# A cached-attention kernel on one core: the PE loop begins with the scores, half of K's transposes move, and ScalarE issues the first loads of x and wq

## The chip, the cores and the metric

The kernel runs on one core of a Trainium2 chip. The metric is the device time of one execution in microseconds (us). A core has five instruction queues: TensorE (PE: matmuls, and PEld, its weight loads), ScalarE (ACT), VectorE (DVE), GpSimd (POOL) and SyncE (SP). DMA transfers are started by SP and ACT here, each in a queue of its own (q1 for SP, q10 for ACT), and carried out by 16 DMA engines that both share.

## The reference

There are two independent blocks, A and B, with the same shapes: B = 16 batches, Sq = 64, D = 640, H = 32 heads, Sk = 512 cached keys, Dh = 128, all bf16.

```python
q = (x @ wq).reshape(B, Sq, H, Dh).transpose(0, 2, 1, 3)
scores = einsum("bhqd,bhkd->bhqk", q, k_cache) * Dh ** -0.5
p = softmax(scores, axis=-1)
o = einsum("bhqk,bhkd->bhqd", p, v_cache)
out = o.transpose(0, 2, 1, 3).reshape(B, Sq, H * Dh) @ wo      # A and B side by side
```

K and V are 268 MB of the 292 MB that are read.

## The kernel before

**Packs.** The work is cut into 128 packs, n = 0 to 127: four heads of two batches each, so 1 MB of K and 1 MB of V. Four packs (j = 0 to 3) make a group g for one pair of batches; eight groups make a phase of 32 packs; two phases do one block. For each pack the engines do, by the names in the code:

- PE: QP projects q (20 matmuls), S makes the scores (32), TR transposes the normalised probabilities (32), PV multiplies with V (128, or 64 where j = 3), OP multiplies with wo (8). XT transposes x once in a group (5).
- ACT: QE copies q out of PSUM, EX takes the exponentials of the four heads with their row sums, OE copies PV's result, ZO clears the sums; XE copies x out of PSUM.
- DVE: KT transposes K, two instructions for a pack (KT0 and KT1 below, line 617), RC takes the reciprocals of the row sums (RC0 for three heads, RC1 for the fourth, line 659), TE copies the transposed probabilities out of PSUM (two, line 696), OS adds the output up.
- POOL: NM normalises the probabilities with the reciprocals, one instruction for a head (line 675), WP rearranges wq for one pack position j (line 575), XC copies x.T (line 592). In the last pack NM runs on DVE.
- SP: LDK (four DMAs of 256 KB, line 552), LDV (two of 512 KB, lines 563 and 565), LDX, LDWQ, and LDWO in the first phase. ACT issues the later LDWO and the stores.

**Order.** Nothing is reordered at run time. `build_plan` gives each operation a due time, the pack number plus an offset from the table `AT` in units of a pack (lines 34 to 36). Each engine's program is its operations sorted by due time (line 169), and the dependences follow the same order (lines 172 to 189): an operation waits for the latest earlier writer of what it reads, and for the earlier readers of what it writes. So an offset that moves past another changes an engine's order; one that does not, changes nothing. SP's own order comes from a separate key (the `loads` list).

In a steady pack PE does S(n), TR(n-1), OP(n-2), QP(n+1), PV(n-1). DVE does TE(n-1), RC0(n), RC1(n), then KT0(n+2) and KT1(n+2), then TE(n).

**The loop.** PE's program is a prologue, a loop of 32 turns of four packs each, and an epilogue (`run_program`, lines 796 to 819); the other engines are unrolled. A turn begins with QP(4k) and ends with OP. A turn holds 821 matmuls, with a weight load each. At the loop's start a part of the steady order has no data yet: packs -2 and -1 are dummies over zeroed buffers (VZ, BZ and WZ on DVE, lines 134 to 136, and the memsets that stand for TE(-2), line 694, and NM(-1), line 666).

**Buffers.** K has a ring of six packs, V a ring of four, the transposed K one of two. So the load of V(n) waits for PV(n-4), and the load of K(n) for S(n-6). x has a single buffer.

**The start.** SP issues x of group 0, wq for j = 0 (640 KB in rows of 1 KB), K(0), wq for j = 1, K(1), and so on. wq is needed by WP(j) on POOL, whose order is WP(0), XC(0), WP(1), NM(-1), WP(2), NM(0), WP(3), NM(1).

**The end.** A flag shows whether a softmax without maxima was safe; `If_ne` then runs a second, general program, which these inputs do not need.

Of the kernel before, what the change touches and what calls it, by code (L numbers as in the profile page):

```python
# [6 lines left out]
F32 = mybir.dt.float32  # L7
# [13 lines left out]
class Cfg:  # L21
# [9 lines left out]
    BASE = 32  # L31
    KLEAD = 2.5
    WIDE = (0, 1, 2)
    AT = dict(XT=-2.485, XE=-2.28, XC=-0.9, QP=-0.45, QE=-0.24, KT=(-1.24, -1.0), S=0,
              EX=(0.21, 0.32, 0.43, 0.54), RC=(0.53, 0.75), NM=(0.56, 0.69, 0.82, 0.95), NMZ=(0.54, 0.55, 0.56, 0.76), TR=1.2,
              TE=(1.26, 1.39), PV=1.75, OE=(2.0, 2.06), ZO=2.11, OP=2.31, OS=2.545, LDWO=2.6, ST=3.374, WP0=-1.75, WP1=-1.6)


class Op:
# [19 lines left out]
def build_plan(dims, cfg, general):  # L59
# [6 lines left out]
    N = NPH * PH  # L66
    AT = cfg.AT
    ops = []
    loads = []
# [8 lines left out]
    def add_output(n):  # L78
        g, j = n // NJ, n % NJ
        final = n >= 0 and dims["FINAL"](g // NBP)  # L80
        for b in range(2):
            tv = n + AT["PV"]
            op = add("sp", "LDV", (n, b), tv - 0.3, [], [("v" if n >= 0 else "absent", n % cfg.NV, b)])
            loads.append((n - cfg.NV + AT["PV"] + 0.2 if n >= 0 else -99.0, 3, op))
        if n > -2:
            add("pe", "TR", n, n + AT["TR"], [("pn", i) for i in range(4)] + [("ident",)], [("B", 4), ("B", 5)])
        for b in range(2):
            add("dve", "TE", (n, b), n + AT["TE"][b], [], [("B", 4 + b), ("pT", b)])
        add("pe", "PV", n, n + AT["PV"], [("pT", 0), ("pT", 1), ("v", n % cfg.NV, 0), ("v", n % cfg.NV, 1)],
            [("B", 4), ("B", 5), ("B67",)])  # L90
        add("act", "OE", (n, 1), n + AT["OE"][0], [], [("B67",), ("oT", 1)])
        add("act", "OE", (n, 0), n + AT["OE"][1], [], [("B", 4), ("B", 5), ("oT", 0)])
        add("act", "ZO", n, n + AT["ZO"], [("zeros",)], [("B67",)])
        add("pe", "OP", n, n + AT["OP"], [("oT", 0), ("oT", 1), ("wo", j)], [("B67",)])
        if j == NJ - 1:
            bp = g % NBP
            add("dve", "OS", g, n + AT["OS"], [("acc", bp)], [("B67",), ("out_sb",) if final else ("acc", bp)])
            if final:
                add("act", "ST", g, n + AT["ST"], [("out_sb",)], [("out_dram", g)])
# [4 lines left out]
    for g in range(N // NJ + 1):  # L104
        n0 = g * NJ
        txt = n0 + AT["XT"]
        add("pe", "XT", g, txt, [("xn", g % cfg.NXN), ("ident",)], [("SB", 0)])
        if g == N // NJ:
            break
        if dims["FIRST"](g // NBP):  # L110
            add("act", "XE", g, n0 + AT["XE"], [], [("SB", 0), ("xs", g % NBP)])
            op = add("sp", "LDX", g, txt - 0.5, [], [("xn", g % cfg.NXN)])
            loads.append((txt - 3.7 if g else -7.0, 0, op))
        add("pool", "XC", g, n0 + AT["XC"], [("xs", g % NBP)], [("xT", g % cfg.NX)])
    for ph in range(NPH):
        twp = [ph * PH + j + (AT["WP1"] if ph else AT["WP0"]) for j in range(NJ)]
        for kt in range(dims["KT"] if ph else 0):
            ready = twp[-1] - PH + 0.5 if ph > 1 else NJ - 1 + AT["WP0"] + 0.5
            op = add("sp", "LDWQ", (ph, kt), twp[0] - 0.5, [], [("ws", kt, j) for j in range(NJ)])
            loads.append((ready + 0.5 + 0.5 * kt if ph == 1 else ready + 2.0 + 0.14 * PH * kt, 1, op))  # L120
        for j in range(NJ):
            w = ph * NJ + j
            n0 = ph * PH + j
            add("pool", "WP", w, twp[j], [("ws", kt, j) for kt in range(dims["KT"])], [("wqp", j)])
            if not ph:
                op = add("sp", "LDWQ", (0, j), twp[j] - 0.5, [], [("ws", kt, j) for kt in range(dims["KT"])])
                loads.append((0.9 * j - 5.2, 1, op))
            if ph:
                add("act", "LDWO", w, n0 - NJ + AT["LDWO"], [], [("wo", j)])
            else:  # L130
                loads.append((n0 - 1.9, 4, add("sp", "LDWO", w, n0 + AT["OP"] - 0.8 * NJ, [], [("wo", j)])))
# [3 lines left out]
    add("dve", "BZ", 0, -9.8, [], [("B", 4), ("B", 5), ("B67",)])  # L135
    add("dve", "WZ", 0, -9.7, [], [("wo", NJ - 2), ("wo", NJ - 1)])
    add("pool", "NM", -1, -1 + AT["NM"][3], [], [("pn", i) for i in range(4)])
    for n in range(-2, N):
        add_output(n)
        if n < 0:  # L140
            continue
        g, j = n // NJ, n % NJ
        add("pe", "QP", n, n + AT["QP"], [("xT", g % cfg.NX), ("wqp", j)], [("SB", 1)])
        add("act", "QE", n, n + AT["QE"], [], [("SB", 1), ("qs", n % cfg.NQ)])
        for i in range(4):
            op = add("sp", "LDK", (n, i), n + AT["KT"][0] - 0.9, [], [("kn", n % cfg.NK)])
            loads.append((n - cfg.NV + AT["PV"] + 0.2 - cfg.KLEAD, 2, op))
        for b in range(2):
            tk = n + AT["KT"][b]
            add("dve", "KT", (n, b), tk, [("kn", n % cfg.NK)], [("kt", n % cfg.NKT, b)])  # L150
        add("pe", "S", n, n + AT["S"], [("qs", n % cfg.NQ), ("kt", n % cfg.NKT, 0), ("kt", n % cfg.NKT, 1)],
            [("SB", i) for i in range(4)])
        for i in range(4):
            h = 4 * n + i
            te = n + AT["EX"][i]
            if general:
                add("dve", "MX", h, te - 0.002, [], [("SB", i), ("negmax", h % 4)])
            add("act", "EX", h, te, [("negmax", h % 4)] if general else [],
                [("SB", i), ("p", h % cfg.NP), ("rs", h)])
            add("pool" if n < N - 1 else "dve", "NM", h, n + (AT["NM"] if n < N - 1 else AT["NMZ"])[i], [("p", h % cfg.NP), ("recip", n % cfg.NR, i // 3)], [("pn", i)])  # L160
        for a in range(2):
            add("dve", "RC", (n, a), n + AT["RC"][a], [("rs", 4 * n + i) for i in ((0, 1, 2), (3,))[a]],
                [("recip", n % cfg.NR, a)])
# [25 lines left out]
                   and not (d.dma and op.dma and d.eng == op.eng)]  # L189

    pe = progs["pe"]
    lo = next(i for i, o in enumerate(pe) if o.kind == "QP" and o.idx == 0)
    hi = next(i for i, o in enumerate(pe) if o.kind == "QP" and o.idx == cfg.PERIOD)
    size = hi - lo
    last_qp = max(o.idx for o in pe[lo:hi] if o.kind == "QP")
    reps = 1 + (N - 1 - last_qp) // cfg.PERIOD
    step = dict(XT=cfg.PERIOD // NJ, QP=cfg.PERIOD, S=cfg.PERIOD, TR=cfg.PERIOD, PV=cfg.PERIOD, OP=cfg.PERIOD)
    for k in range(reps):
        for i in range(size):
# [5 lines left out]
    for op in ops:  # L205
        if op.kind == "OP":
            at[("OE", (op.idx, 1))].deps += [d for d in op.deps if d.kind in ("LDWO", "WZ")]
            op.deps = [d for d in op.deps if d.kind not in ("LDWO", "WZ")]
        if op.kind == "XT" and op.idx > 0:
            at[("EX", 4 * (NJ * op.idx - NJ + 1))].deps += [d for d in op.deps if d.kind == "LDX"]  # L210
            op.deps = [d for d in op.deps if d.kind != "LDX"]
        if op.kind == "QP" and op.idx > 0:
            at[("EX", 4 * op.idx - 4)].deps += [d for d in op.deps if d.kind == "WP"]
            op.deps = [d for d in op.deps if d.kind != "WP"]

    own = {"XC", "QE", "KT", "NM", "TE", "OE", "ZO", "OS", "LDV"}

# [45 lines left out]
    counts = dict(base)  # L263

    def sem_key(op):
        if op.kind == "LDV":
            return ("d_v", op.writes[0][1])
        if op.kind in LOADS:
# [160 lines left out]
def mha_kernel(nc, blocks, out, cfg=None):  # L429
# [23 lines left out]
    with contextlib.ExitStack() as es:  # L453
# [24 lines left out]
        recip = sb("recip", [128, NR, 4], F32)  # L478
        ident = sb("ident", [128, 128], BF16)
        extreme = sb("extreme", [128, 4], F32)  # L480
        good = sb("good", [128, 1], BF16)
        flag = sb("flag", [1, 1], I32)
        ps = es.enter_context(nc.psum_tensor("ps", [128, 8, 512], F32))

        sems = []
        for p, (_progs, counts, _loop) in enumerate(plans):
            sems.append({key: es.enter_context(nc.semaphore("_".join([f"p{p}"] + [str(k) for k in key])))
# [124 lines left out]

        def em_KT(e, op):
            n, a = op.idx
            dst = kt_ring[:, n % NKT, 16 * a:16 * a + 16].rearrange("p t j b k two -> p (t j) b (k two)").bitcast(F32)
            src = kn_ring[:, n % NK, a, :].bitcast(F32).rearrange("p (c h b l) -> p c h b l", h=8, b=2, l=2)
            ins = e.transpose(dst.rearrange("p c b (h l) -> p c h b l", h=8, l=2), src)  # L617
# [73 lines left out]
        def em_TE(e, op):  # L691
            n, b = op.idx
            if n == -2:
                ins = e.memset(pT_sb[:, b].rearrange("p t q -> p (t q)"), 0.0)
                return ins, ins
            ins = e.tensor_copy(pT_sb[:, b].rearrange("p t q -> p (t q)"), pt_bank(b))  # L696
            return ins, ins
# [80 lines left out]
        def emit(e, op, p, taken):  # L778
# [4 lines left out]
                attach = waits.pop()  # L783
            for s, v in waits:
                e.wait_ge(sem[s], v * units(s))
            kind = "EXG" if p and op.kind == "EX" else op.kind
            first, last = emitters[kind](e, op)
            if last is None:
# [119 lines left out]
```

## Time and profile before

| | |
|---|---|
| median of 8 runs | 749.31 us (748.43 to 751.14) |
| the profiled execution | 750.81 us, span 749.1 us |
| PE busy | 684.5 us (91%) |
| DVE, ACT, POOL busy | 527.6, 519.3, 405.3 us |
| HBM read | 292.03 MB, 393 GB/s over the span |
| idle of POOL before NM | 316.2 us, waiting for RC |
| idle of DVE before KT | 99.3 us, waiting for K's DMA |

The span is cut into 40 slices of 18.7 us. A line of digits gives an engine's busy share of each slice in tenths. The chain of waits is read from the end backwards: what released each step. Its pieces stand here in the order of time as "start, length, engine, tile, line, count"; "issue" is time in which nothing that the profile shows was waited for. SPq is SP's issuing.

### The profile page before, as it was taken

Reading aid. Unit: us, or ns where it says so; the run is one execution under the profiler, and the core shown is the slowest. Engines: PE = TensorE matmul, PEld = TensorE weight load, DVE = VectorE, ACT = ScalarE, POOL = GpSimd, SP = SyncE. Lnnn points to the kernel's source line nnn. Section 1 sums busy time; section 2 is a strip of 40 time slices with the busy share of each in tenths; the row PEclk is TensorE's granted clock in tenths of the full one; section 3 lists DMA queues with packets and bytes.
Section 4 is the critical chain, followed back from the end, with each engine's and each line's share of the span. In section 5 each row is a group of like instructions: output and inputs, shape, how many; then the busy total and the mean of one; then the engine's idle time right before and its main releaser. Section 6 shows DMA issues by size and latency. Waiting matters only on the chain.

```text
span 749.1 us, 57618 instructions
## 1 busy us (share of the span) xinstructions
PE 684.5 (91%) x26518; PEld 532.8 (71%) x26518; DVE 527.6 (70%) x818; ACT 519.3 (69%) x1559; POOL 405.3 (54%) x580
## 2 busy tenths in 40 slices
PE   4679999999999999999988999999998899999995
PEld 2447777777777767767766777777776677877773
DVE  7337777777777777677756777777675787787863
ACT  2337787877767677767766777777776677777772
POOL 5425556555874554545774455455486455555550
PEclk9869999999999999999999999999999999999996
DMA  8999999999999999999999999999999999999960
GB/s 317 399 402 410 411 411 413 411 411 412 407 399 414 412 414 411 413 412 413 413 398 407 411 412 413 412 410 410 413 408 401 411 413 412 412 413 411 409 267 14
DMA packets 87518, 295.15 MB, mean 394 GB/s; under 512 B 13360, under 2 KB 28208, under 8 KB 71088
## 3 DMA queue, kind: packets, MB, share of 16 engines
q1 hardware_dynamic: 78832, 284.22, 94.9%
q10 hardware_dynamic: 8640, 10.49, 3.9%
q14 instruction: 37, 0.30, 0.1%
q8 instruction: 9, 0.15, 0.1%
HBM read 292.03 MB, written 2.62 MB: 393 GB/s over the span
## 4 chain that ended last, share of the span: by engine, by line
PE 39%; SPq 27%; DMA 12%; POOL 7%; ACT 6%; DVE 5%; issue 5%; ACTq 0%; DVEq 0%
SPq L552 18%; PE ps L710 10%; PE ps L730 10%; PE ps L603 8%; DMA kn_ring<-in_B_k_cache_dram 8%; POOL pn_sb L675 7%; PE ps L627 5%; SPq L563 5%; PE ps L686 5%; ACT p_ring L646 3%; SPq L565 3%; DMA v_ring<-in_B_v_cache_dram 2%; DMA kn_ring<-in_A_k_cache_dram 2%; DVE kt_ring L617 2%; ACT oT_sb L718 2%
## 5 line engine op out<-in xcount | busy, mean ns | idle before, releaser
L675 POOL TENSOR_SCALAR pn_sb<-p_ring,recip 128x512 bf16<-128x512 bf16 x508 | 343.1, 697 | 316.2 <-DVE recip L659 316.2
L617 DVE STREAM_TRANSPOSE kt_ring<-kn_ring 128x1024 f32<-128x1024 f32 x256 | 302.8, 1222 | 99.8 <-DMA kn_ring<-in_B_k_cache_dram 76.2
L646 ACT ACTIVATE p_ring<-ps 128x512 bf16<-128x512 f32 x512 | 298.7, 598 | 20.6 <-PE ps L627 6.1
L696 DVE COPY pT_sb<-ps 128x1024 bf16<-128x1024 bf16 x258 | 164.7, 679 | 74.8 <-PE ps L686 74.2
L710 PE MATMUL ps<-pT_sb,v_ring 32*128 32x64 bf16 (+1 forms) x14528 | 162.8, 192 | 25.5 <-DVE pT_sb L696 7.1
L710 PEld LDWEIGHTS ps<-pT_sb,v_ring 32*128 32x128 bf16 (+1 forms) x14528 | 146.4, 92 | 41.1 <-issue 22.6
L730 PE MATMUL ps<-wo_sb,oT_sb 128*128 128x320 bf16 x1040 | 169.3, 307 | 5.0 <-issue 3.9
L603 PE MATMUL ps<-xT_ring,wqp_sb 128*128 128x128 bf16 x2560 | 166.4, 221 | 5.7 <-POOL xT_ring L592 5.5
L603 PEld LDWEIGHTS ps<-xT_ring,wqp_sb 128*128 128x128 bf16 x2560 | 158.0, 114 | 12.5 <-issue 5.8
L718 ACT ACTIVATE oT_sb<-ps 128x256 bf16<-128x256 f32 x260 | 85.7, 381 | 114.3 <-PE ps L710 114.3
L627 PE MATMUL ps<-kt_ring,qs_ring 32*64 32x512 bf16 x4096 | 140.9, 386 | 0.0
L609 ACT ACTIVATE qs_ring<-ps 128x512 bf16<-128x512 f32 x128 | 76.5, 598 | 82.1 <-PE ps L603 82.1
L686 PEld LDWEIGHTS ps<-ident,pn_sb 64*128 64x128 bf16 x4128 | 70.9, 96 | 76.0 <-ACT ps L722 44.3
L730 PEld LDWEIGHTS ps<-wo_sb,oT_sb 128*128 128x128 bf16 x1040 | 92.7, 99 | 44.3 <-issue 4.5
L646 ACT ACTIVATION_READ_ACCUMULATOR p_ring<-ps 128x1 f32 x512 | 106.2, 207 | 0.0
L686 PE MATMUL ps<-ident,pn_sb 64*128 64x64 bf16 x4128 | 84.8, 192 | 18.2 <-POOL pn_sb L675 11.6
L627 PEld LDWEIGHTS ps<-kt_ring,qs_ring 32*64 32x64 bf16 x4096 | 54.0, 104 | 28.9 <-issue 1.6
L659 DVE RECIPROCAL recip<-rowsum 128x3 f32<-128x3 f32 (+1 forms) x256 | 40.6, 163 | 35.1 <-ACT p_ring L646 30.4
L722 ACT ACTIVATE ps<-zeros 128x256 f32<-128x256 bf16 x130 | 51.3, 395 | 0.0
L575 POOL COPY wqp_sb<-ws_sb 128x1280 bf16<-128x1280 bf16 x32 | 39.3, 1261 | 6.5 <-DMA ws_sb<-in_A_wq_dram 6.5
L592 POOL COPY xT_ring<-xs_sb 128x640 bf16<-128x640 bf16 x32 | 23.1, 723 | 1.7 <-PE ps L603 1.7
L582 PE MATMUL ps<-ident,xn_ring 128*128 128x128 bf16 x165 | 14.9, 222 | 4.4 <-DMA xn_ring<-in_A_x_dram 3.5
(26 smaller groups left out, 65.8 us busy)
## 6 DMA issues: line engine op xcount, KB each, us to landing
kn_ring<-in_A_k_cache_dram SPq DMA_DIRECT2D x256, 256.0 KB
v_ring<-in_A_v_cache_dram SPq DMA_DIRECT2D x128, 512.0 KB, 11.2
kn_ring<-in_B_k_cache_dram SPq DMA_DIRECT2D x256, 256.0 KB
v_ring<-in_B_v_cache_dram SPq DMA_DIRECT2D x128, 512.0 KB, 13.1
ws_sb<-in_B_wq_dram SPq DMA_DIRECT2D x10, 512.0 KB, 16.0
wo_sb<-in_B_wo_dram ACTq DMA_DIRECT2D x8, 640.0 KB, 14.4
ws_sb<-in_A_wq_dram SPq DMA_DIRECT2D x4, 640.0 KB, 7.1
wo_sb<-in_A_wo_dram SPq DMA_DIRECT2D x4, 640.0 KB, 13.7
```

The costliest lines, as they stand in the source:

```text
L552: ins = e.dma_start(kn_ring[2 * b + l::4, n % NK].rearrange("p a c -> p (a c)"), src)
L603: last = e.matmul(ps[:, 1, f * 128:(f + 1) * 128], w[:, kt, f, :], xT_ring[:, xs, kt, :], start=(kt == 0), stop=(kt == KT - 1))
L609: ins = e.activation(qs_ring[:, op.idx % NQ].rearrange("p f b q -> p (f b q)"), ps[:, 1, :], ACTF.Copy, scale=scale)
L617: ins = e.transpose(dst.rearrange("p c b (h l) -> p c h b l", h=8, l=2), src)
L627: last = e.matmul(ps[64 * b:64 * b + 64, i, :], qs_ring[rows, n % NQ, f, b, :], kt_ring[rows, n % NKT, :, f // 2, b, :, f % 2], start=(f = ...
L646: ins = e.activation(dst, src, ACTF.Exp, scale=1.0, accum_out=rowsum[:, h:h + 1])
L675: ins = e.tensor_scalar(dst, src, recip[:, h // 4 % NR, i:i + 1], 1.0, ALU.mult, ALU.mult)
L686: last = e.transpose(pt_bank(b)[:, 64 * c:64 * c + 64], pn_sb[rows, c, :], ident[rows, rows], tile_position=(64 * b, 0))
L696: ins = e.tensor_copy(pT_sb[:, b].rearrange("p t q -> p (t q)"), pt_bank(b))
L710: last = e.matmul(ps[:, 4 + i, 64 * b:64 * b + 64], v_ring[rows, n % NV, b, c, :], pT_sb[rows, b, c, :], start=(t == 0 and i < 2), stop=(t ...
L718: ins = e.activation(oT_sb[:, 2 * a:2 * a + 2, :], o_ps[:, 2 * a:2 * a + 2, :], ACTF.Copy)
L730: last = e.matmul(out_ps[:, s, :], oT_sb[:, i, :], wo_sb[:, 4 * j + i, s * NH0:(s + 1) * NH0], start=(j == 0 and i == 0), stop=(j == NJ - ...
```

## The change

Three things change, and the due times with them.

1. The PE loop's turn is found from S(0) to S(4), not from QP(0) to QP(4). So QP(0) moves into the prologue; a turn ends with QP(4k+4) and PV; and since the last turn has such a QP too, a projection QP(128) is computed that nobody reads, with an XC(32) on POOL and two one-column memsets in `spare` on DVE that stand for KT(128). PV(-2) is left out, and the two memsets of pT (TE(-2)) become one-column memsets in `spare`.
2. KT's offsets go from (-1.24, -1.0) to (-0.672, -0.375). Sorted with the other new offsets, DVE's steady order becomes TE(n-1), RC0(n), KT1(n+1), RC1(n), KT0(n+2), TE(n). PE's and POOL's steady orders are the same as before.
3. The first x and the four wq loads of phase 0 go from SP's queue to the head of ACT's. SP begins with K(0). Later loads of x and wq stay with SP.

In the last pack the offsets of NM on DVE are now (0.626, 1.242, 1.729, 1.805), against 1.293 for TR. So TR(127) waits for the first two heads' NM only, and reads for the other two heads what pack 126 left in `pn_sb`; their NM comes later.

```diff
-    AT = dict(XT=-2.485, XE=-2.28, XC=-0.9, QP=-0.45, QE=-0.24, KT=(-1.24, -1.0), S=0,
-              EX=(0.21, 0.32, 0.43, 0.54), RC=(0.53, 0.75), NM=(0.56, 0.69, 0.82, 0.95), NMZ=(0.54, 0.55, 0.56, 0.76), TR=1.2,
-              TE=(1.26, 1.39), PV=1.75, OE=(2.0, 2.06), ZO=2.11, OP=2.31, OS=2.545, LDWO=2.6, ST=3.374, WP0=-1.75, WP1=-1.6)
+    AT = dict(XT=-2.555, XE=-2.383, XC=-0.788, QP=-0.428, QE=-0.224, KT=(-0.672, -0.375), S=0,
+              EX=(0.252, 0.307, 0.358, 0.616), RC=(0.572, 0.794), NM=(0.803, 0.854, 1.088, 1.187),
+              NMZ=(0.626, 1.242, 1.729, 1.805), TR=1.293, TE=(1.432, 1.47), PV=1.701, OE=(1.888, 2.013), ZO=2.221,
+              OP=2.387, OS=2.576, LDWO=2.6, ST=3.542, WP0=-1.75, WP1=-1.596)
...
-            add("dve", "TE", (n, b), n + AT["TE"][b], [], [("B", 4 + b), ("pT", b)])
-        add("pe", "PV", n, n + AT["PV"], [("pT", 0), ("pT", 1), ("v", n % cfg.NV, 0), ("v", n % cfg.NV, 1)],
-            [("B", 4), ("B", 5), ("B67",)])
+            add("dve", "TE", (n, b), n + AT["TE"][b], [], [("B", 4 + b), ("pT", b)] if n > -2 else [])
+        if n > -2:
+            add("pe", "PV", n, n + AT["PV"], [("pT", 0), ("pT", 1), ("v", n % cfg.NV, 0), ("v", n % cfg.NV, 1)],
+                [("B", 4), ("B", 5), ("B67",)])
...
-            op = add("sp", "LDX", g, txt - 0.5, [], [("xn", g % cfg.NXN)])
-            loads.append((txt - 3.7 if g else -7.0, 0, op))
+            if g:
+                loads.append((txt - 3.7, 0, add("sp", "LDX", g, txt - 0.5, [], [("xn", g % cfg.NXN)])))
+            else:
+                add("act", "LDX", g, -21.0, [], [("xn", g % cfg.NXN)])
...
-                op = add("sp", "LDWQ", (0, j), twp[j] - 0.5, [], [("ws", kt, j) for kt in range(dims["KT"])])
-                loads.append((0.9 * j - 5.2, 1, op))
+                add("act", "LDWQ", (0, j), j - 20.0, [], [("ws", kt, j) for kt in range(dims["KT"])])
...
         add("pe", "QP", n, n + AT["QP"], [("xT", g % cfg.NX), ("wqp", j)], [("SB", 1)])
+        if n == N:
+            for b in range(2):
+                add("dve", "KT", (n, b), n + AT["KT"][b])
+            break
...
-    lo = next(i for i, o in enumerate(pe) if o.kind == "QP" and o.idx == 0)
-    hi = next(i for i, o in enumerate(pe) if o.kind == "QP" and o.idx == cfg.PERIOD)
-    size = hi - lo
-    last_qp = max(o.idx for o in pe[lo:hi] if o.kind == "QP")
-    reps = 1 + (N - 1 - last_qp) // cfg.PERIOD
+    lo = next(i for i, o in enumerate(pe) if o.kind == "S" and o.idx == 0)
+    size = next(i for i, o in enumerate(pe) if o.kind == "S" and o.idx == cfg.PERIOD) - lo
+    reps = N // cfg.PERIOD
...
             n, a = op.idx
+            if n == NH // 4:
+                ins = e.memset(spare[:, 4 * current[0] + a:4 * current[0] + a + 1], 0.0)
+                return ins, ins
...
             if n == -2:
-                ins = e.memset(pT_sb[:, b].rearrange("p t q -> p (t q)"), 0.0)
+                ins = e.memset(spare[:, 4 * current[0] + 2 + b:4 * current[0] + 3 + b], 0.0)
```

More of the change, by code (lines that the diff above doesn't have):

```diff
@@ L107, in build_plan @@
         add("pe", "XT", g, txt, [("xn", g % cfg.NXN), ("ident",)], [("SB", 0)])
-        if g == N // NJ:
-            break
-        if dims["FIRST"](g // NBP):
+        if g < N // NJ and dims["FIRST"](g // NBP):
             add("act", "XE", g, n0 + AT["XE"], [], [("SB", 0), ("xs", g % NBP)])
-            op = add("sp", "LDX", g, txt - 0.5, [], [("xn", g % cfg.NXN)])
-            loads.append((txt - 3.7 if g else -7.0, 0, op))
+            if g:
+                loads.append((txt - 3.7, 0, add("sp", "LDX", g, txt - 0.5, [], [("xn", g % cfg.NXN)])))
+            else:
+                add("act", "LDX", g, -21.0, [], [("xn", g % cfg.NXN)])
         add("pool", "XC", g, n0 + AT["XC"], [("xs", g % NBP)], [("xT", g % cfg.NX)])
@@ L137, in build_plan @@
     add("pool", "NM", -1, -1 + AT["NM"][3], [], [("pn", i) for i in range(4)])
-    for n in range(-2, N):
-        add_output(n)
+    for n in range(-2, N + 1):
+        if n < N:
+            add_output(n)
         if n < 0:
@@ L214, in build_plan @@
             op.deps = [d for d in op.deps if d.kind != "WP"]
+    if general:
+        at[("QP", 0)].deps += [at[("KT", (0, b))] for b in range(2)]
     own = {"XC", "QE", "KT", "NM", "TE", "OE", "ZO", "OS", "LDV"}
@@ L265, in sem_key @@
     def sem_key(op):
+        if op.kind in ("LDX", "LDWQ") and op.eng == "act":
+            return ("d_first",) + op.writes[0]
         if op.kind == "LDV":
@@ L480, in mha_kernel @@
         extreme = sb("extreme", [128, 4], F32)
+        spare = sb("spare", [128, 8], F32)
         good = sb("good", [128, 1], BF16)
@@ L483, in mha_kernel @@
         ps = es.enter_context(nc.psum_tensor("ps", [128, 8, 512], F32))
+        current = [0]
         sems = []
@@ L785, in emit @@
                 e.wait_ge(sem[s], v * units(s))
+            current[0] = p
             kind = "EXG" if p and op.kind == "EX" else op.kind
```

## The prediction

> **What bounds the kernel now.** First the page's slices, for the DMA engines:
>
> ```profile
> DMA  8999999999999999999999999999999999999960
> GB/s 317 399 402 410 411 411 413 411 411 412 407 399 414 412 414 411 413 412 413 413 398 407 411 412 413 412 410 410 413 408 401 411 413 412 412 413 411 409 267 14
> ```
>
> DMA is full from the second slice to the 38th, at 398 to 414 GB/s. PE is at 90% or more in most slices too, so two limits lie close together, and the chain of waits must say which holds where. Its last wait for a DMA:
>
> ```profile
> 568.15 19.47 DMA kn_ring<-in_B_k_cache_dram
> ...
> 587.64 2.37 DVE kt_ring L617 x2
> 590.02 1.17 DVE pT_sb L696 x2
> 591.19 0.14 DVE recip L659 x2
> ...
> 591.36 2.71 POOL pn_sb L675 x4
> ```
>
> From 215 to 588 us the chain runs mostly through SP's issuing and K's landings: the end of this stretch is set by bytes. K(n+2) lands, and DVE, in order, does KT0 and KT1 before TE(n), the next reciprocals and NM. After 588 the chain holds compute alone: 161 us to the end, 20.9 us per turn, with K just in time (DVE waits 0.6 us for it at 598 and 603, 0.2 to 0.5 us after 700). So three things count: when DMA begins and whether it ever runs dry; what stands between the last late K and the chain behind it; and the tail:
>
> ```profile
> 731.13 1.30 DVE pT_sb L696 x2
> ...
> 732.56 1.27 PE ps L710 x128
> ...
> 735.12 1.00 issue
> 736.12 0.29 PE ps L686 x7
> ...
> 737.88 1.90 PE ps L710 x64
> ...
> 740.80 2.33 PE ps L730 x8
> ```
>
> TR(127) stops for 1.00 us after 25 of 32 matmuls with nothing to wait for, and then PV and OP take 1.90 and 2.33 us instead of their usual 1.1 and 1.2. The table of stretches shows why: the granted clock drops.
>
> ```profile
> 736.00:737.00 1.00, 0.88 (x12) 0.68 (x13) 0.56 (x1) 0.00 (x0) 0.00 (x0) 1.00 0.00 0
> 737.00:738.00 1.00, 0.99 (x11) 0.36 (x10) 1.00 (x3) 0.00 (x0) 0.00 (x0) 0.60 0.00 0
> ```
>
> The stop has a pattern. In the first turn the chain has the same stops:
>
> ```profile
> 18.16 2.15 issue
> ...
> 26.28 2.09 issue
> ...
> 32.18 3.05 issue
> ```
>
> Counted in the timeline, 127 matmuls (254 instructions) lie between each two, and packets of a queue named "instruction" land beside them: PE fetches its program in blocks. Five blocks end stalls, at 20.31, 28.37, 35.23, 41.52 and 49.52 us, 7.3 us apart on average. From 60 to 730 us that queue is still: the loop stays resident. The stop at 735.12 is the next block, 153 matmuls behind the loop's end.
>
> **The change, part by part.** The sum is made against the profiled execution, 750.81 us with a span of 749.1; it lies 1.5 us above the median of 749.31, to which I apply the differences. From no change, 0.2% (1.5 us) can be told.
>
> *Head: DMA's start.* SP's five moved issues took 0.39, 0.42, 0.58, 0.58 and 0.59 us.
>
> ```profile
> 2.00:3.00 1.00, 0.00 (x0) 0.00 (x0) 1.00 (x1) 0.08 (x1) 0.00 (x0) 1.00 0.81 208
> 3.00:4.00 1.00, 0.54 (x5) 0.45 (x5) 1.00 (x1) 0.00 (x0) 0.00 (x0) 1.00 0.54 130
> ```
>
> DMA was idle 0.19 and 0.46 us here, and some 0.2 us more up to 13 us, since SP issued too slowly. With two queues issuing this 0.8 us mostly goes: 0.7 us gained.
>
> *Head: wq's place.* ACT's queue now competes with SP's. The nearest case is ACT's wo load beside SP's K and V, in 199 to 204 us:
>
> ```profile
> q1 hardware_dynamic: 363, 1.54, 77.6%
> q10 hardware_dynamic: 364, 0.47, 25.7%
> ```
>
> Packets alternate one for one, whatever their size. A K packet has 8 KB (0.32 us at 411/16 GB/s), one of wq 1 KB (about 0.05 us, from 84 ns per packet in the first 16 us). wq(0) and wq(1) with x are 91 packets per engine; beside them pass 91 of SP's (three packs of K with 24 large packets, x, V(0), most of wo): 17 us, so wq(1) lands near 20 us, where POOL had it at 10.94. WP(1) 2.45 and NM(-1) 1.81 follow, then TR(-1) and OP(-2), near 25 us. There PE enters its second block, at 14.5 us before. From there blocks rule: 7.0 us to the first arrival, then 7.3 each. PV(1), which frees V's slot for V(5), now needs four arrivals instead of five: about 54 us instead of 50.1, and PV(2) 61.7 instead of 57.2. QP(0), S(0) and ACT's table load and XE, which stand behind the five issues (2.6 us), end before TR(-1); the memsets of pT (1.02 us) and PV(-2) (1.90) that fall away lie in the same hidden stretch.
>
> Can DMA wait that long? By 50.1 us SP had issued 20.4 MB (8 packs of K, 5 of V, wo, wq, three x, two parts of the next wq), and 18.4 MB had moved: 5.0 us in hand, 5.4 us at 57.25. Less 1.0 us from issue to first bytes and the 0.7 gained, PE may be late by 3.3 and 3.7 us; it is late by some 3.9 and 4.5. DMA runs dry for about 0.8 us. The head's sum is +0.1; I take +0.2. Bounds: -0.7 if wq(1) lands 3 us earlier, +3 if it lands 3 us later. [...]
>
> *KT.* KT0(n+2) stays directly behind RC1(n) and ahead of TE(n), as before; only KT1 moves, past TE(n) and RC0(n+1). In the chain at 587.64 one of two transposes (1.19 us of 2.37) leaves: -1.2. What is late next? KT1(n+2) must end before S(n+2): in the turn's tightest pack RC0 starts at 106.65, OS ends at 107.53, KT1 at 108.78, plus 0.14 from DVE to PE, and S starts at 109.07: 0.15 us to spare. RC1 now waits for KT1, and with it the fourth NM: 108.94 becomes 109.05, with TR at 110.07 held by OE. Bounds: -1.4, and +0.5 if the 0.15 us is missed by 0.1 in the last six turns.
>
> *Turn boundary.* Before, OP's eight long matmuls (1.26 us) run while PE updates semaphores and branches; QP follows OP after 1.10 us there as in every pack. Now a turn ends with PV, whose 256 instructions take 1.15 us, so little lies queued to cover the branch. S(4k) opens the pack whose NM bounds the turn, so a gap counts. Bounds: nothing (the old boundary), and 0.2 us, the longest unexplained gap before S's weight loads. I take 0.1, the middle: six turns after 605 us, +0.6. [...]
>
> *Tail.* QP(128) now precedes PV(126): PV starts 2.31 us after OP(125)'s 731.02, as in a steady pack, at 733.33 instead of 732.56, +0.77. XC(32) ends near 731.1 and delays nothing; the two one-column memsets hide in DVE's 3.05 us of idle. NM's new place hides too: before, the last NM ended at 733.91 and OE at 734.51. Against that, the loop's end moves 20 matmuls on, so the next block begins 133 behind it, and TR, OP, PV, OP need only 112: the 1.00 us stop goes. TR starts at 735.34 and takes 0.57; OP(126) starts at 735.95 instead of 736.40. PE is then idle 0.8 and 0.3 us in these 4 us instead of 2.0, so I expect the clock to hold: PV 1.1, OP 1.2. OE 0.66 and ZO as before: OS starts near 740.95 instead of 743.22, -2.3. Bounds: -2.4; +0.8 if stop and clock stay.
>
> Sum: 0.2 - 1.2 + 0.6 - 2.3 = -2.7, so 746.6 us (748.1 for the profiled execution).
>
> **The rivals.**
>
> *Gains cancel.* The clock drops all the same, or PE meets the K that is just in time (0 to 0.6 us of slack after 588) and gives KT's gain back. For it: DVE's waits at 598 to 723. Against: KT0 alone needs half as long. The tail is then -0.5 and KT about 0: 0.2 + 0 + 0.6 - 0.5 = +0.3, 749.6.
>
> *wq too late* (slower). PE reaches PV(1) 10 us late, not 4: DMA is dry for 6.5 us. Price: 6.5 - 0.7 - 1.2 + 0.6 - 2.3 = +2.9, 752.2. It decides from 7.1 us of lateness on, where it eats the 3.6 us that the other terms bring. For it: one-for-one packets and wq's small rows. Against: V's ring is full by then, so SP stops and wq gets the engines alone.
>
> *The loop no longer stays resident.* Its end lies only 8 matmuls before a block boundary now (28 before). If crossing it evicts the first block, every turn pays at least one stop of 2.1 us: 32 x 2.1 = 67 us, 816.
>
> *The change does not do what it says* in part: of K's transposes only KT1 moves; that is in the sum.
>
> **How the numbers follow.** My forecast has 0.58 (its own range 744.3 to 748.0); gains cancel 0.24; wq too late 0.15; loop 0.03. Range at 8 in 10: 744.3, where all low bounds meet (-0.7 - 1.4 + 0 - 2.4 gives 744.8) with 0.5 us for the scatter of the runs, to 751.0, between the cancelled case and the late one. Faster takes the forecast and a little of the cancelled case, 0.60; same 0.20; slower, late wq, the loop and the rest, 0.20.
>
> **What will show it.** POOL's second WP near 20 us; the DMA share under 0.9 somewhere in 50 to 65 us if wq is late. Behind the last late K, one KT ahead of TE. TR(127) without a stop and the last PV near 1.1 us. PE idle between PV and S once per turn of at most 0.2 us. Wrong would be: a stall in every turn, S waiting for KT1 in steady turns, or a clock of 0.5 before the last OP.

## The result and the profile after

The changed kernel takes 752.94 us in the median (751.95 to 754.28), the kernel before 749.87 us beside it: a ratio of 1.0041, with a 95% interval of 1.0032 to 1.0050. That is 3.1 us slower, where 2.7 us faster had been forecast. The profiled execution took 752.95 us, with a span of 751.2.

First the slices of the page, the same two lines as before the change:

```profile
DMA  8999999999999999999999999999999999999960
GB/s 320 391 402 409 411 411 413 411 411 404 383 401 413 411 415 411 414 412 415 411 403 403 410 412 413 412 411 410 412 405 402 414 413 413 414 412 414 411 247 14
```

DMA is as full as it was, but for a dip to 383 GB/s in the 11th slice (407 before), and in each microsecond from 44 to 68 us its share stays at 0.97 or more. So nothing is lost to a dry head. What is lost shows in PE's order of time. A line gives start, length, engine, line, operation, tiles and count, and in brackets the idle time ahead of it with what the profile takes for its releaser. Here are the end of one pack and the end of one turn:

```profile
93.72 1.22 PE L724 MATMUL ps<-pT_sb,v_ring 32*128 32x64 bf16 x128
94.87 1.07 PE L641 MATMUL ps<-kt_ring,qs_ring 32*64 32x512 bf16 x32
...
98.92 1.22 PE L724 MATMUL ps<-pT_sb,v_ring 32*128 32x64 bf16 x128
101.00 1.07 PE L641 MATMUL ps<-kt_ring,qs_ring 32*64 32x512 bf16 x32 [0.87 <-ACT oT_sb L732]
```

Inside a turn, S starts 1.15 us behind PV's start; at the end of a turn, 2.08 us. PE stands still for 0.87 us in between, in every turn. In the kernel before, the same place lies between OP and QP, and there is no gap: 1.10 us from start to start, as in every other pack.

```profile
95.11 1.26 PE L730 MATMUL ps<-wo_sb,oT_sb 128*128 128x320 bf16 x8
96.21 1.28 PE L603 MATMUL ps<-xT_ring,wqp_sb 128*128 128x128 bf16 x20
```

A turn that nothing but PE holds up, measured from one group's transposes of x (XT) to the next, takes 21.64 to 21.66 us after the change; before it was 20.72. I call this the floor. It is 0.93 us higher, over 32 turns. Yet the time grew by 3.1 us, not by 30. XT(26) and XT(32) show where the difference lands, first before the change, then after:

```profile
595.88 0.44 PE L582 MATMUL ps<-ident,xn_ring 128*128 128x128 bf16 x5
...
721.62 0.44 PE L582 MATMUL ps<-ident,xn_ring 128*128 128x128 bf16 x5
```

```profile
594.05 0.44 PE L593 MATMUL ps<-ident,xn_ring 128*128 128x128 bf16 x5
...
725.43 0.44 PE L593 MATMUL ps<-ident,xn_ring 128*128 128x128 bf16 x5
```

At XT(26) the changed kernel is 1.8 us ahead. It had fallen 5.3 us behind by 282 us (XT(12)) and caught up by 413 us, since in that middle stretch the kernel before waits for K (DVE 28.2 us from 282 to 413 us, after the change 2.8); PE's gaps fall into waits that were there anyway. From XT(26) on DMA hardly sets the pace (in both kernels the six turns together lie only 1.4 to 1.5 us above six floors), and they take 131.4 us instead of 125.7: 5.6 us, or 6 x 0.93. The tail from XT(32) to the end of the span takes 25.8 us instead of 27.5. So -1.8 + 5.6 - 1.7 = +2.1, the difference of the spans (751.2 and 749.1).

The chain behind a late K has one transpose ahead of TE, as forecast:

```profile
514.02 13.79 DMA kn_ring<-in_B_k_cache_dram
527.81 0.02 issue
527.83 1.25 DVE kt_ring L631
529.08 1.17 DVE pT_sb L710 x2
530.25 0.09 DVE recip L673
```

In the tail, TR(127) does not stop, and PV and OP keep their usual lengths, with the granted clock at 1.00 throughout:

```profile
739.16 0.64 PE L700 MATMUL ps<-ident,pn_sb 64*128 64x64 bf16 x32 [0.79 <-ACT oT_sb L732]
739.74 1.26 PE L744 MATMUL ps<-wo_sb,oT_sb 128*128 128x320 bf16 x8
741.28 1.11 PE L724 MATMUL ps<-pT_sb,v_ring 64*128 64x64 bf16 x64 [0.28 <-DVE pT_sb L710]
743.42 1.26 PE L744 MATMUL ps<-wo_sb,oT_sb 128*128 128x320 bf16 x8 [1.03 <-ACT ps L736]
```

And the waits view (us in total, times, longest) puts new waits down to two other engines and to PE's own sequencer (PEq):

```profile
PE ps L641 <- ACT oT_sb L732: 23.4, 27, 0.9
...
PEld ps L641 <- DVE kt_ring L631: 18.9, 20, 1.0
...
PEld ps L641 <- PEq L830: 9.5, 10, 1.0
...
PE ps L641 <- PEq L830: 2.6, 3, 0.9
```

S does not read `oT_sb` at all: of ACT it waits for QE, which had ended at 99.62 us (from 99.02 for 0.60 us), and of DVE for KT1, which had ended 0.56 us before S started (from 99.22 for 1.22 us, S at 101.00). Line 830, which the same view names for 3 of the gaps of PE and 10 of the weight loads', is PE's own: it is the semaphore subtraction of the loop in the code. That is a hint; what makes the gap had to be tested.

**Theory.** The turn's end itself is the gap. There PE's sequencer works through four semaphore subtractions (of ACT's, DVE's, POOL's and one of V's counts), the loop's addition, the branch and two waits. Ahead of it stood OP, 16 instructions in 1.26 us; now PV stands there, 256 instructions in 1.22 us. That OP's are issued well before they have run, and PV's are not, is an assumption of mine; no trace shows the issuing. **Rival A**: the late wq and ScalarE's loads cost the time. **Rival B**: S waits for the KT1 that has moved.

Below, a ratio is that of a run's kernel to the kernel before, measured beside it. In the changed kernel and in e1, e3, e4, e5, e10 and e11, TR(127) reads for two of the last pack's four heads what pack 126 left, as told above; e2, e6, e7, e8, e9 and e12 have all four NM ahead of it. In the kernels of the first list these two heads enter the output with the probabilities of another pack; a kernel that is to be used needs all four NM ahead of TR(127). This has no weight in the times: in e8 the fourth NM ends 1.32 us behind the start of PV(126), and in e1 TR(127) starts 2.00 us behind it, held by OE.

### The profile page after: what moved, and what is told of

The parts are those of the page before. It is cut to its first block, busy times and chain, and to the rows that moved or that the text cites. A ratio compares the mean times of both kernels' runs of the same rounds, so it can differ in the third digit from the quotient of the medians.

```text
span 751.2 us, 57532 instructions
## 1 busy us (share of the span) xinstructions
PE 677.8 (90%) x26410; PEld 530.3 (71%) x26410; DVE 516.7 (69%) x820; ACT 520.2 (69%) x1559; POOL 406.0 (54%) x581
## 4 chain that ended last, share of the span: by engine, by line
PE 54%; SPq 11%; ACT 10%; POOL 10%; DMA 9%; issue 4%; DVE 2%; ACTq 0%; DVEq 0%
PE ps L724 13%; PE ps L744 13%; PE ps L614 12%; POOL pn_sb L689 9%; PE ps L641 9%; SPq L563 7%; PE ps L700 7%; ACT p_ring L660 6%; ACT oT_sb L732 4%; DMA kn_ring<-in_B_k_cache_dram 4%; DMA v_ring<-in_B_v_cache_dram 3%; SPq L574 2%; DMA ws_sb<-in_A_wq_dram 2%; SPq L576 1%; PE ps L593 1%
## 5 line engine op out<-in xcount | busy, mean ns | idle before, releaser
L631 DVE STREAM_TRANSPOSE kt_ring<-kn_ring 128x1024 f32<-128x1024 f32 x256 | 310.6, 1226 | 52.5 <-DMA kn_ring<-in_B_k_cache_dram 51.3
L744 PE MATMUL ps<-wo_sb,oT_sb 128*128 128x320 bf16 x1040 | 166.6, 304 | 3.4 <-issue 2.4
L724 PE MATMUL ps<-pT_sb,v_ring 32*128 32x64 bf16 (+1 forms) x14400 | 159.3, 192 | 11.2 <-issue 6.0
L724 PEld LDWEIGHTS ps<-pT_sb,v_ring 32*128 32x128 bf16 (+1 forms) x14400 | 142.8, 92 | 25.5 <-issue 7.0
L641 PEld LDWEIGHTS ps<-kt_ring,qs_ring 32*64 32x64 bf16 x4096 | 55.6, 104 | 56.9 <-DVE kt_ring L631 18.9
L673 DVE RECIPROCAL recip<-rowsum 128x3 f32<-128x3 f32 (+1 forms) x256 | 37.4, 146 | 6.4 <-ACT p_ring L660 0.4
## 6 DMA issues: line engine op xcount, KB each, us to landing
kn_ring<-in_B_k_cache_dram SPq DMA_DIRECT2D x256, 256.0 KB, 12.2
```

Of the source, the lines that this page charges most:

```text
L641: last = e.matmul(ps[64 * b:64 * b + 64, i, :], qs_ring[rows, n % NQ, f, b, :], kt_ring[rows, n % NKT, :, f // 2, b, :, f % 2], start=(f = ...
L724: last = e.matmul(ps[:, 4 + i, 64 * b:64 * b + 64], v_ring[rows, n % NV, b, c, :], pT_sb[rows, b, c, :], start=(t == 0 and i < 2), stop=(t ...
L744: last = e.matmul(out_ps[:, s, :], oT_sb[:, i, :], wo_sb[:, 4 * j + i, s * NH0:(s + 1) * NH0], start=(j == 0 and i == 0), stop=(j == NJ - ...
```

## The experiments: which part costs

**e1: the rotation alone undone.**

```diff
-    lo = next(i for i, o in enumerate(pe) if o.kind == "S" and o.idx == 0)
-    size = next(i for i, o in enumerate(pe) if o.kind == "S" and o.idx == cfg.PERIOD) - lo
-    reps = N // cfg.PERIOD
+    lo = next(i for i, o in enumerate(pe) if o.kind == "QP" and o.idx == 0)
+    hi = next(i for i, o in enumerate(pe) if o.kind == "QP" and o.idx == cfg.PERIOD)
...
```

> The changed kernel, but PE's turn begins with QP again, as before; due times, K's transposes and ScalarE's loads stay changed. Theory (the end of the turn, bare behind PV's short matmuls, costs 0.9 us in each of the turns): the turn's floor returns from 21.66 to 20.73 us, PE has no gap of 0.87 us ahead of the first S of a turn, TR(127)'s stop of 1.0 us comes back; K's transpose -1.2, head +0.5, so 749 us (748 to 750.5). Rival A (late wq and ScalarE's loads cost the time): stays at 752 to 753. Rival B (S waits for the KT1 that has moved): stays at 752 to 753 with S waiting for DVE in most turns.

Measured: 747.88 us, ratio 0.9974 (0.9962 to 0.9986). The floor is 20.71 us, no S waits. Rivals A and B fall: their parts of the change are all in this kernel. Undoing the rotation is worth 1.0041 / 0.9974, 5.0 us, and this kernel is faster than both.

**e2: the rotation alone made**, on the kernel before (with QP(0) waiting for the first K, which its order of waits needs).

```diff
-    lo = next(i for i, o in enumerate(pe) if o.kind == "QP" and o.idx == 0)
...
+    lo = next(i for i, o in enumerate(pe) if o.kind == "S" and o.idx == 0)
+    size = next(i for i, o in enumerate(pe) if o.kind == "S" and o.idx == cfg.PERIOD) - lo
...
+    at[("QP", 0)].deps += [at[("KT", (0, b))] for b in range(2)]
```

> The kernel before with the turn from S alone (QP(128) and its stand-ins included); due times, K's transposes and loads as before. In the last pack all four NM come ahead of TR(127). Theory: floor near 21.65 us, gap of 0.9 us ahead of S in every turn, nothing of K's gain, tail -2 us: 752 to 754 us. Rivals A and B: no loss, the tail's gain remains: 747 to 748.5 us.

Measured: 753.19 us, ratio 1.0045 (1.0032 to 1.0057), as the theory has it. The floor is 21.53 us and the gap 0.75, 0.11 less than in the changed kernel. There S waits for ACT's count alone; with KT1 moved behind TE it waits for DVE's too, one instruction more (the four subtractions are the same in both). So part 2 of the change seems to have a small price in the open gap as well; no run moves this wait alone.

**e6 and e7: the other two parts alone**, on the kernel before.

```diff
-    AT = dict(XT=-2.485, XE=-2.28, XC=-0.9, QP=-0.45, QE=-0.24, KT=(-1.24, -1.0), S=0,
+    AT = dict(XT=-2.485, XE=-2.28, XC=-0.9, QP=-0.45, QE=-0.24, KT=(-1.0, -0.36), S=0,
```

> The kernel before with KT's offsets alone, (-1.0, -0.36): KT1(n+1) between RC0 and RC1, KT0(n+2) ahead of TE(n), as in the changed kernel; loads, turn and all else as before. The prediction's term: -1.2 us, so 748.4 us (bounds -1.4 to +0.5: 748.2 to 750.1), DVE's idle ahead of KT near 50 us instead of 99. Rival: the loop is set by DMA and K's place is worth nothing, 749.6 us.

Measured: 748.58 us, ratio 0.9983 (0.9975 to 0.9992), so -1.3 us (-1.9 to -0.6). XT(26) comes at 594.7 instead of 595.9 us, but in e7, where KT stays, it comes at 595.0 too, so this place does not show the gain by itself. The gain is as forecast, but the sign in the waits that was expected is not there:

```profile
DVE kt_ring L617 <- DMA kn_ring<-in_B_k_cache_dram: 103.1, 64, 4.0
DVE kt_ring L617 <- DMA kn_ring<-in_A_k_cache_dram: 42.5, 28, 3.0
```

DVE waits 145.6 us for K, more than the 99.3 of before: it reaches K earlier and waits longer. The 52.2 us of the changed kernel are no gain of KT's; there PE is slower, and K has landed by the time DVE wants it. e1, with KT moved and PE's floor at 20.71 us, waits 145.0 us.

```diff
+            else:
+                add("act", "LDX", g, -21.0, [], [("xn", g % cfg.NXN)])
...
+                add("act", "LDWQ", (0, j), j - 20.0, [], [("ws", kt, j) for kt in range(dims["KT"])])
```

> The kernel before with the first x and the four wq on ScalarE's queue alone. The prediction's term: +0.2 us (bounds -0.7 to +3), so 749.8 us, the second WP near 16 us as in the changed kernel. Rival (the first bytes come earlier, and DMA never runs dry): -0.7 to -0.9 us, 748.8 us. Rival A (late wq costs the time): 752 us.

Measured: 749.62 us, ratio 0.9995 (0.9986 to 1.0004). The loads make no difference that can be told. The three parts one by one add up to +0.45 - 0.17 - 0.05 = +0.23%, the whole change is +0.41%; the second wait in the gap, if it costs 0.11 us in six turns, is 0.1% of that, and the rest lies within the intervals.

## The experiments: what the turn's end is made of

**e3, e4, e11: fewer and more instructions at the turn's end.** e3 moves three subtractions from there to places behind OP; e11 the fourth, too; e4 adds four more.

```diff
-    take = {}
-    for s in sorted(per, key=str):
+    take = {("q_act",): spots[0], ("q_dve",): spots[1], ("q_pool",): spots[2]}
+    for s in sorted(set(per) - set(take), key=str):
```

> The changed kernel with three of the four semaphore subtractions that stand at the turn's end (those of ACT's, DVE's and POOL's counts) moved behind the turn's first three OPs. Theory, if the subtractions make up the gap in equal parts with the branch (four subtractions, the loop's addition, the branch and S's waits over 0.9 us, some 0.1 us each): gap 0.55 to 0.65 us, floor 21.3 to 21.4, and since DMA then sets more of the turns again, 748.5 to 751 us. If the branch alone makes the gap: gap 0.87, 752 to 753.5 us. Rivals A and B: 752 to 753.5 us, too, with a smaller gap or not.

```diff
+                for i in range(4):
+                    e.sem_inc(s_pad, 1 - i % 2 * 2)
             taken = {s: v * reps for s, v in per.items()}
```

> The changed kernel with four more semaphore instructions at the turn's end (+1 and -1 twice on a semaphore that nobody waits for). Theory at some 0.1 us each: gap 1.2 to 1.4 us, floor 22.0 to 22.1 us, and since PE sets nearly all turns, 32 x 0.4 = 12.8 us more, less what the last DMA-bound turns absorb: 758 to 766 us. If the branch alone makes the gap: 753 us with a gap of 0.9 us.

```diff
+    base["d_v", 2] = 4
...
+    last = [s for s, _ in turn[-1].waits if s[0] == "d_v"][0]
+    take[last] = spots[3]
...
+            e.sem_inc(sems[p]["d_v", 2], 4 * 16)
```

> As e3, and the fourth subtraction (of V's DMA count) moved from the turn's end behind the fourth OP; that count starts 4 higher for it. Only the loop's addition, the branch and S's two waits are left at the turn's end. Theory at 0.16 us for one: gap 0.25 us, floor 21.02, and 749.5 to 750.5 us (e5 had the same floor and 749.83). If the gap does not shrink below e3's 0.41: 751.0 us.

The first S of a turn, in e11, e3 and e4:

```profile
99.95 1.07 PE L644 MATMUL ps<-kt_ring,qs_ring 32*64 32x512 bf16 x32 [0.26 <-issue]
```

```profile
99.31 1.07 PE L641 MATMUL ps<-kt_ring,qs_ring 32*64 32x512 bf16 x32 [0.41 <-DVE kt_ring L631]
```

```profile
101.33 1.07 PE L641 MATMUL ps<-kt_ring,qs_ring 32*64 32x512 bf16 x32 [1.49 <-ACT ps L736]
```

| kernel | semaphore instructions at the turn's end | gap, us | floor, us | XT(26) to XT(32), us | time, us | ratio |
|---|---|---|---|---|---|---|
| e11 | 0 | 0.26 | 21.05 | 127.0 | 748.71 | 0.9979 (0.9971 to 0.9988) |
| e3 | 1 | 0.41 | 21.18 | 128.3 | 751.01 | 1.0015 (1.0006 to 1.0024) |
| changed kernel | 4 | 0.86 | 21.64 | 131.4 | 752.94 | 1.0041 (1.0032 to 1.0050) |
| e4 | 8 | 1.49 | 22.26 | 134.2 | 764.34 | 1.0189 (1.0176 to 1.0203) |

The gap is a straight line: 0.26 us and 0.154 us for each semaphore instruction (1.23 us over eight). The four subtractions are 0.62 of the 0.86 us, more than the equal shares of about 0.1 us that were expected before e3. The time is no straight line, since what the DMA-bound middle can absorb ends: e4's floor lies above DMA's pace almost everywhere, and it reaches XT(26) 5.2 us late. Moving the four subtractions, with all else of the change in place, takes back 0.62%, 4.6 us.

The three lines also name three different releasers, `issue`, DVE and ACT, for the same gap. The profile names the semaphore event that came last before the gap ended; as the gap grows, it ends behind other events. A releaser that changes with the length of the wait is no cause.

No run here shows the branch alone; e11's 0.26 us are the addition, the branch and two waits together. The four semaphore subtractions, 0.62 us, are the larger part.

**e5: the same four instructions where OP covers them**, on e1.

```diff
+                for i in range(4):
+                    e.sem_inc(s_pad, 1 - i % 2 * 2)
             taken = {s: v * reps for s, v in per.items()}
```

> The kernel of e1 (turn from QP, the rest as changed) with e4's four extra semaphore instructions at the turn's end. Theory: a turn's end takes 0.95 us, of which OP's eight long matmuls (1.26 us) cover all; with four more at 0.157 us each (e4: +0.63 for four) it takes 1.58 us and sticks out by 0.3 to 0.5 us: PE's floor 21.0 to 21.2 us instead of 20.71, and DMA takes up most of it: 748.5 to 751 us. Rival (semaphore instructions cost PE their time wherever they stand, and e4 shows no cover): floor 21.34, 751 to 752.5 us. If OP covers even 1.58 us: floor 20.7, 747.9 us.

```profile
95.30 1.26 PE L734 MATMUL ps<-wo_sb,oT_sb 128*128 128x320 bf16 x8
96.75 1.28 PE L607 MATMUL ps<-xT_ring,wqp_sb 128*128 128x128 bf16 x20 [0.19 <-issue]
```

Measured: floor 21.01 us, 749.83 us, ratio 1.0000 (0.9990 to 1.0011). QP starts 1.45 us behind OP instead of 1.10. With eight instructions at its end the turn's floor is 21.01 us behind OP (0.30 more than e1's) and 22.26 behind PV (e4). OP hides 1.25 us more than PV does, about as long as its eight matmuls run (1.26 us). And 6 x 0.30 = 1.8 us on e1's 747.88 comes close to what was measured (749.83): again it is mostly the last six turns that pay.

**e10: the turn from PV**, so that QP ends it.

```diff
-    lo = next(i for i, o in enumerate(pe) if o.kind == "S" and o.idx == 0)
-    size = next(i for i, o in enumerate(pe) if o.kind == "S" and o.idx == cfg.PERIOD) - lo
+    lo = next(i for i, o in enumerate(pe) if o.kind == "PV" and o.idx == -2)
+    size = next(i for i, o in enumerate(pe) if o.kind == "PV" and o.idx == cfg.PERIOD - 2) - lo
```

> The changed kernel with the turn from PV(-2), so that it ends with QP: 20 matmuls, 1.28 us, in 40 instructions. PV(-2) and the memsets of pT are back; QP(128) stays. Theory (what counts is how long the matmuls run that are queued behind the sequencer): if PE takes all of QP into its queue, the 0.95 us are hidden, floor 20.7 to 20.8 us, no gap ahead of PV; 748.0 to 749.0 us, with QP(128)'s 0.77 us in the tail. If the queue holds only a few matmuls of 64 ns: a gap of 0.3 to 0.7 us ahead of PV, floor 21.0 to 21.4, 749.5 to 752 us.

```profile
95.62 1.28 PE L613 MATMUL ps<-xT_ring,wqp_sb 128*128 128x128 bf16 x20
96.83 1.22 PE L723 MATMUL ps<-pT_sb,v_ring 32*128 32x64 bf16 x128
```

Measured: floor 20.71 us, no gap, 748.79 us, ratio 0.9978 (0.9967 to 0.9988). QP covers the turn's end. It had less to cover than was expected, though: the kernel places the subtractions anew for each turn, and here DVE's and V's stand behind an OP, so only two of the four are left at the turn's end. By the line above these two, with the addition, the branch and the waits, would be a gap of 0.57 us behind PV (an estimate); behind QP there is none. QP's matmuls take 64 ns each and those of PV 9 ns, so it is not the length of the group that counts (1.28 and 1.22 us). That QP and OP are issued faster than they run, and PV is not, fits all of this; no run shows the issuing itself.

## The experiments: the tail

e1 kept the stop in TR(127), and yet ended 26.2 us behind XT(32), against 27.5 before the change:

```profile
733.15 0.52 PE L690 MATMUL ps<-ident,pn_sb 64*128 64x64 bf16 x23 [0.79 <-ACT oT_sb L722]
735.09 0.32 PE L690 MATMUL ps<-ident,pn_sb 64*128 64x64 bf16 x9 [1.42 <-issue]
735.34 1.26 PE L734 MATMUL ps<-wo_sb,oT_sb 128*128 128x320 bf16 x8
```

Here the granted clock held, at 1.00 from 730 to 740 us. **e8 and e9** move the stop, by more instructions ahead of the loop; 24 more transposes of the first x in e8, 23 in e9.

```diff
-            for kt in range(KT):
+            for kt in [i % KT for i in range(24 if op.idx == 0 else 0)] + list(range(KT)):
                 last = e.transpose(x_ps[:, kt * 128:(kt + 1) * 128],
```

> The kernel of e1 with 24 more transposes of the first x in PE's prologue (48 instructions, the same result written again), and with all four NM of the last pack ahead of TR(127). The program moves on by 48 instructions: the stop of 1.42 us in TR(127), 23 matmuls in, should fall ahead of TR, where PE waits 0.79 us for ACT's OE. Theory: -0.8 us against e1, 747.1 us (746.5 to 747.9). If the loop's end, now at the edge of a block, no longer lets the first block stay: 30 stops of 2 us and more, above 800 us. If the stop goes with TR's own instructions and not with the place in the program: as e1, 747.9 us.

> As e8, with 23 more transposes instead of 24 (46 instructions). e8's stop came 127 of 128 matmuls into PV(126), so that ACT's OE waited for the last one, 2.27 us. One matmul less puts the edge of the block behind PV(126), ahead of TR(127). Theory: OE no longer waits, the stop (to about 2.3 us behind PV's end) lies beside OE, and TR starts some 0.8 us behind OE instead of stopping 1.4 us midway: TR(127) at 0.9 us earlier than in e8, 748.3 to 748.8 us, and 747.0 us where the granted clock holds in the tail, as it did in e1. Rival (the place of the stop makes no difference to what follows): 749.6 us as e8.

The end of PV(126) and what follows, in e8 and then in e9:

```profile
730.43 1.20 PE L714 MATMUL ps<-pT_sb,v_ring 32*128 32x64 bf16 x127 [0.28 <-DVE pT_sb L700]
733.90 0.18 PE L714 MATMUL ps<-pT_sb,v_ring 32*128 32x64 bf16 x1 [2.27 <-issue]
```

```profile
730.60 1.21 PE L714 MATMUL ps<-pT_sb,v_ring 32*128 32x64 bf16 x128 [0.28 <-DVE pT_sb L700]
733.93 1.03 PE L690 MATMUL ps<-ident,pn_sb 64*128 64x64 bf16 x32 [2.12 <-issue]
734.90 2.31 PE L734 MATMUL ps<-wo_sb,oT_sb 128*128 128x320 bf16 x8
```

e8: 749.60 us, ratio 0.9998 (0.9989 to 1.0006); e9: 748.54 us, 0.9980 (0.9972 to 0.9989). The place of the stop follows the place in the program, one matmul for one transpose, so the reading of the stops as blocks of code holds. In e8 it caught the last matmul of PV, and OE waited behind it for the whole stop; the shift was one matmul too large, and the 747.1 us that I expected did not come. e9 put it behind PV, and TR starts 0.91 us earlier than in e8, as expected. Neither beats e1, whose stop is shorter: e8 is slower, and e9 cannot be told from it. The loop still stayed resident in both: no turn has a stop of its own.

After the stop e9's clock falls, in the table of stretches (PE, PEld, DVE, ACT and POOL busy, clock, DMA share, GB/s):

```profile
733.00:734.00 1.00, 0.07 (x4) 0.07 (x6) 0.00 (x0) 0.00 (x0) 0.00 (x0) 0.84 0.00 0
734.00:735.00 1.00, 1.00 (x33) 0.91 (x34) 0.00 (x0) 0.00 (x0) 0.00 (x0) 0.50 0.00 0
```

Of the profiled executions with a stop in the tail, five show such a drop before the last OP: to 0.50 in the kernel before, e9 and e10; in e6 and e8 the mean from 735 to 740 us is 0.70 and 0.66, and an OP takes 2.32 and 2.31 us. Three do not (e1, e5, e7: 1.00 from 730 to 740 us, and OP behind TR takes 1.26 us). Of the six without a stop none does (the changed kernel, e2, e3, e4, e11, e12: 1.00 until the last OP). The drop goes with the stop, but not each time; what decides is open.

**e12: a shorter program**, so that the tail lies within the blocks that are there.

```diff
-    WIDE = (0, 1, 2)
+    WIDE = (0, 1)
```

> The kernel of e1 with V of pack position j = 2 in the layout that j = 3 has (WIDE = (0, 1): packets of 2 KB instead of 4 KB, PV in 64 matmuls instead of 128), and all four NM of the last pack ahead of TR(127). PE's program becomes 128 instructions shorter in the loop and 128 in what follows, so the tail should stay within the resident blocks: no stop in TR(127), clock at 1.00 to the last OP. A narrow PV takes 0.12 us less, but TR behind it waits 0.19 us for POOL's NM: floor 20.7 to 20.8. If 2 KB packets cost DMA nothing: tail -0.8 us against e1, 746.5 to 747.5 us, the best of all. If the smaller packets cost DMA 1% on an eighth of its bytes: +0.9 us, 747.5 to 749 us; a DMA rate below 405 GB/s in the middle of the run would show it.

```profile
733.86 1.11 PE L714 MATMUL ps<-pT_sb,v_ring 64*128 64x64 bf16 x64 [0.28 <-DVE pT_sb L700]
735.72 0.64 PE L690 MATMUL ps<-ident,pn_sb 64*128 64x64 bf16 x32 [0.75 <-ACT oT_sb L722]
736.29 1.26 PE L734 MATMUL ps<-wo_sb,oT_sb 128*128 128x320 bf16 x8
```

```profile
GB/s 326 390 402 408 407 410 411 407 411 408 404 394 412 409 413 409 408 411 411 410 396 404 409 408 410 409 408 408 407 407 397 409 412 410 408 411 412 406 371 26
```

Measured: 749.65 us, ratio 0.9990 (0.9981 to 0.9999), above both ranges that were expected. The stop is gone, and the tail behind XT(32) takes 24.9 us instead of e1's 26.2. But with the smaller packets of V the slices 12 to 20 have 408.6 GB/s in the mean and the slices 22 to 30 have 407.8, where e1 has 411.0 and 410.4:

```profile
GB/s 324 391 402 411 411 412 413 410 413 411 408 396 416 412 414 410 413 414 412 412 398 408 409 412 414 410 411 409 412 409 401 410 413 413 409 415 413 409 318 19
```

That is 0.6% less, and XT(32) comes 2.7 us later than in e1: the gain in the tail is lost before it, most likely to DMA. e1 has the lowest time of this study, but e9, e10 and e11 (ratios of 0.9978 to 0.9980) lie within its interval.

## Why the prediction was wrong, step by step

**The turn boundary: wrong, and it decided.** The step that failed is "Bounds: nothing (the old boundary), and 0.2 us, the longest unexplained gap before S's weight loads. I take 0.1, the middle: six turns after 605 us, +0.6." The place and the six turns were right, and the reason (PV leaves little queued to cover the end of the turn) fits the runs, though none shows the queue; the size was wrong. It measured 0.93 us a turn, so +5.6 us. With that one term exchanged, the sum is 0.2 - 1.2 + 5.6 - 2.3 = +2.3, 753.1 us for the profiled execution, which took 752.95. The upper bound was drawn from gaps in a program in which the work in question was hidden; such rows say nothing of its length. The instructions were there to be counted in the code: the forecast took 0.1 us for the branch and left out the four subtractions, which measured 0.154 us each.

**Head: right in sum, for other reasons.** +0.2 us was forecast, e7 shows -0.4 (-1.0 to +0.3). DMA's start won little or nothing of the 0.7 us: 249 GB/s in the first 10 us in both kernels, and 257 in e1 and e7, which is worth 0.2 us. And wq was less late than worked out. The packets of the two queues did not alternate one for one from the start: from 4 to 10 us ACT's moved 919 and SP's 177; from 10 to 14 us it was 260 and 260. POOL's two WP in the changed kernel:

```profile
8.14 2.45 POOL L586 COPY wqp_sb<-ws_sb 128x1280 bf16<-128x1280 bf16 x2 [6.57 <-DMA ws_sb<-in_A_wq_dram]
...
16.36 2.45 POOL L586 COPY wqp_sb<-ws_sb 128x1280 bf16<-128x1280 bf16 x2 [5.12 <-DMA ws_sb<-in_A_wq_dram]
```

The second starts at 16.36 us, not near 20. PE's stops in the first turn then came early enough: V(5) was issued at 49.21 us, against 50.12 before and some 54 in the forecast, and DMA did not run dry there (a share of 0.97 or more from 44 to 68 us). The rival "wq too late" named 752.2 us and so came near the measured number, by a mechanism that did not take place: with the same late wq, e1 takes 747.88.

**KT: right in size.** -1.2 us forecast, -1.3 in e6, and the chain has one transpose ahead of TE; that the gain arises there is not shown apart. The fear that S would miss KT1 by 0.1 us in steady turns did not come true; the price of KT1's place seems to be one wait instruction in the gap, 0.11 us.

**Tail: right in its mechanism, and right in size against this one execution.** From OP(125)'s start to OS it took 9.9 us instead of 12.2, the -2.3 of the forecast; from XT(32) to the end it is -1.7. The difference lies behind OS, 6.4 us to the end of the span instead of 5.9; in the other runs it is 5.8 to 6.5. But the profiled execution of before was one in which the clock fell. With a stop and no drop (e1) the tail is 26.2 us, and there the change gains 0.4.

**The loop** stayed resident, as was held likely: of the two queues named "instruction", the one whose packets land beside PE's stops (q8) moved 6 up to 60 us and none from 60 to 730 us, before and after the change; and the changes did what they said.

## What to carry to other kernels

What the loop's end cost here depended on what stood ahead of it: behind PV's 256 short instructions PE stood still for 0.87 us a turn, behind OP's 16 long ones not at all (1.10 us from OP to QP, as in every pack). So look first for a place behind few, long instructions, and count every semaphore instruction (0.154 us here), and the addition, branch and waits (0.26 us together), before a loop's end is moved behind many short ones. Price such work by an experiment or by counting, not by gaps of a program in which it is covered. The cost in every turn was paid here only where PE set the pace, in 6 turns of 32 (5.6 us), while the DMA-bound middle gave the rest back.

## What was not expected of the hardware

- A semaphore instruction of PE that nothing covered took 0.154 us (e11, e3, the changed kernel and e4 on one line); addition, branch and two waits together 0.26 us.
- Eight matmuls of OP (1.26 us) hid 1.25 us more of it than 128 of PV did (1.22 us; floors of 21.01 us in e5 and 22.26 in e4). Twenty of QP (1.28 us) hid a turn's end with two subtractions in full (e10).
- A stop for a block of code lasted 0.8 to 1.4 us where it fell within TR (six executions) and 2.1 to 2.3 us behind or at the end of PV (e9, e8); the granted clock then fell in five of the eight, to 0.50 in the three that were read microsecond by microsecond (the kernel before, e9, e10).
- With V's packets at 2 KB instead of 4 KB in a quarter of V, DMA's rate in the middle of the run was 0.6% lower (e12: 408.6 and 407.8 GB/s; e1: 411.0 and 410.4).
